# Chunk attention and a Fourier mix beside an MLP: weighting of v and the next tile's scores behind each other

## The chip, the cores and the metric

The kernel runs on one core of one Trainium2 chip. The metric is the device time of one execution in microseconds (us), as a median over several executions. All executions spoken of here were in the fast state. An engine is called by the profile's name where a line is read: PE is TensorE, DVE VectorE, ACT ScalarE, POOL GpSimd, SP SyncE.

## The reference

```python
q, k, v: [8, 8, 576, 64]                        # batch, heads, sequence, head dimension
# attention inside chunks of 64 positions (9 chunks)
scores = scale * q_c @ k_c.T;  scores -= max(scores)
attn = exp(scores);  attn /= sum(attn) + 1e-9
x = (attn @ v_c)  ->  [8, 576, 512]             # heads side by side
# Fourier mix and MLP
u  = x + real(fft(fft(x, axis=1), axis=2))
un = (u - mean(u)) / sqrt(var(u) + 1e-6)        # over the last axis
return u + relu(un @ w_ch1) @ w_ch2             # 512 -> 2048 -> 512
```

## The kernel before

The 4608 rows form 36 tiles of 128 rows. The MLP works on groups of four tiles (0 to 8). Its large products fill TensorE; the attention and the Fourier mix of the next batch run as a *side*, a generator of *steps*. After each *tick* of the MLP loop (16 matmul records of 128x128 by 256, some 3.45 us) the loop takes as many steps as the plan of that batch says. From group 2 on, the first product is computed in halves with seven products instead of eight. The last evictions of one tick free the bank into which the next tick writes, so a late VectorE is a late TensorE (at 464.93 us, 1.04 us of idle time).

```python
def attention(b):
    lo, hi = first[b], first[b + 1] - 1
    ...
    for n in range(lo, hi + 1):
        att_S(n)                   # scores: 32 matmuls of 64x64
        softmax(n)                 # DVE: maximum, subtraction; ACT: exponential
        yield
        if n + 1 < NT and (b > 0 or n < hi):
            att_T(n + 1)           # q and k of the next tile transposed in blocks by DVE
        yield
        if n > lo:
            att_V(n - 1)           # weighting of v: 32 matmuls of 64x64
            if n + 2 < NT:
                load_v(n + 2)
            yield ready(n - 1)
        att_P(n)                   # probabilities transposed by PE, copied by ACT
        yield
    att_V(hi)
    ...

def att_T(n):
    if n >= first[2]:
        for src, dst, nm in ((qs, qT, "qT"), (ks, kT, "kT")):
            a = src.pop(n)...
            t = one_p.tile([128, NJ, 2, CH + 1], FP32, tag=nm, name=nm)
            ...
            nc.vector.transpose(out=to..., in_=a)
        if n + 1 < NT:
            load(n + 1)            # q and k of the tile after it: one buffer each, just read
        return
    ...
```

`load` starts four transfers for q and four for k, or eight and eight where the two halves of a tile come from two batches, all on SyncE's queue. That queue also carries the loads of v, the fetches of weight slabs and this exchange of the first rows of a batch's tiles, whose second half waits until its first half has landed (1.51 us at one place):

```python
def shift(b):
    ...
    eng = nc.gpsimd if b < 2 else nc.sync
    t = three_p.tile([128, XW], FP32, tag="y", name="first")
    for i in range(NM):
        eng.dma_start(out=t[2 * i:2 * i + 2, 0:DM], in_=lows[i][0:CH + 1:CH, 0:DM])
    eng.dma_start(out=t[2 * NM:2 * NM + 1, 0:DM], in_=rest)
    for i in range(NM):
        eng.dma_start(out=lows[i][0:CH + 1:CH, 0:DM], in_=t[2 * i + 1:2 * i + 3, 0:DM])
    eng.dma_start(out=rest, in_=t[0:1, 0:DM])
```

The kernel's PSUM tiles take eight banks: two for transposes, two for one attention tile (scores or weighted tile), four for the MLP's products.

Of the kernel before, what the change touches and what calls it, by code (L numbers as in the profile page):

```python
# [16 lines left out]
def kernel(  # L17
# [32 lines left out]
    nc = tc.nc  # L50
# [230 lines left out]
            free.remove(fit[0])  # L281
            nc.sync.dma_start(out=raw(i).rearrange("p f r -> p (f r)"), in_=pieces[i][1].bitcast(U32))

    def round_weight(i):






        if i < len(pieces):
            w, t = pieces[i][0], raw(i)
            lo, hi, wi = t[:, :, 0], t[:, :, 1], w.bitcast(U32)
            p = power[i] = three_p.tile([128, 512], U32, tag="o", name="power")
            nc.vector.tensor_scalar(wi, hi, 0x000FFFFF, None, ALU.bitwise_and)
            nc.scalar.activation(out=w, in_=wi, func=ACTF.Copy, scale=2.0 ** -20, bias=1.0)
            nc.vector.tensor_scalar(p, hi, 0x7FF00000, None, ALU.bitwise_and)
            nc.scalar.activation(out=p, in_=p, func=ACTF.Relu, scale=-1.0, bias=top[:, 0:1])
            nc.scalar.activation(out=p, in_=p, func=ACTF.Relu, scale=-8.0, bias=top[:, 1:2])
        if 0 < i <= len(pieces):  # L300
            w, t = pieces[i - 1][0], raw(i - 1)
            lo, hi = t[:, :, 0], t[:, :, 1]
            p = power.pop(i - 1)
            nc.vector.scalar_tensor_tensor(w, lo, 2.0 ** -52, w, ALU.mult, ALU.add)
            nc.vector.scalar_tensor_tensor(p, hi, 0x80000000, p, ALU.bitwise_and, ALU.bitwise_or)
            nc.vector.tensor_tensor(out=w, in0=w, in1=p.bitcast(FP32), op=ALU.mult)
            r = raws.pop(i - 1)
            if i - 1 + len(spaces) < N_EARLY or r < N_LATE:
                free.append(r)
            load_weight(max(raws, default=i - 1) + 1)  # L310
# [6 lines left out]
        return pt  # L317


    def att_T(n):  # L320




        if n >= first[2]:
            for src, dst, nm in ((qs, qT, "qT"), (ks, kT, "kT")):
                a = src.pop(n).rearrange("p j (t b d) -> p j t b d", t=4, b=2)[:, :, :, 0]
                t = one_p.tile([128, NJ, 2, CH + 1], FP32, tag=nm, name=nm)
                low = kind(n) == LO and nm == "qT"
                to = t[:, :, :, CH:0:-1] if low else t[:, :, :, 0:CH]  # L330
                if kind(n) == HI:
                    to = to[:, :, ::-1]
                nc.vector.transpose(out=to.rearrange("p j c (r t) -> p j t c r", t=4), in_=a)
                if low:
                    nc.gpsimd.tensor_copy(t[:, :, :, 0:1], t[:, :, :, CH:CH + 1])
                dst[n] = t.rearrange("p j c t -> p (j c) t")
            if n + 1 < NT:
                load(n + 1)
            return
        a = qs.pop(n)  # L340
        pt = turn(lambda j: a[:, 2 * j:2 * j + 2, :].rearrange("p h d -> p (h d)"))
        t = one_p.tile([128, 2 * NJ, CH + 1], FP32, tag="qT", name="qT")
        low = kind(n) == LO
        nc.scalar.copy(t[:, :, CH:0:-1] if low else t[:, :, 0:CH], pt.rearrange("p j (c t) -> p (j c) t", c=2))
        if low and n < first[1]:
            nc.scalar.copy(t[:, :, 0:1], t[:, :, CH:CH + 1])
        elif low:
            nc.gpsimd.tensor_copy(t[:, :, 0:1], t[:, :, CH:CH + 1])
        qT[n] = t
        a2 = ks.pop(n)  # L350
        pt = turn(lambda j: a2[:, 2 * j:2 * j + 2, :].rearrange("p h d -> p (h d)"))
        t = one_p.tile([128, NJ, 128], FP32, tag="kT", name="kT")
        nc.scalar.copy(t, pt)
        kT[n] = t.rearrange("p j (c t) -> p (j c) t", c=2)
        if first[1] <= n + 1 < NT:
            load(n + 1)
# [17 lines left out]
    def softmax(n):  # L374
        sc = scs.pop(n)
        s4 = sc[:, :, 0:NJ * CH].rearrange("p e (j k) -> p e j k", j=NJ)
        mx = sm_p.tile([128, 2, NJ], FP32, tag="mx", name="mx")
        nc.vector.tensor_reduce(out=mx, in_=s4, axis=AX.X, op=ALU.max)
        ex = two_p.tile([128, NJ, 2, CH], FP32, tag="ex", name="ex")
        nc.vector.tensor_tensor(  # L380
            out=ex.rearrange("p j e k -> p e j k"),
            in0=s4,
            in1=mx.unsqueeze(3).to_broadcast([128, 2, NJ, CH]),
            op=ALU.subtract,
        )
        nc.scalar.activation(out=ex, in_=ex, func=ACTF.Exp, scale=scale)
        es[n] = ex

    def att_P(n):
        ex = es.pop(n)  # L390
# [5 lines left out]
    def att_V(n):  # L396
        a, b = pT.pop(n), vs.pop(n)
        if n < first[1]:
            xp = early_xp
        else:  # L400
            xp = ps_a.tile([128, 2, 512], FP32, tag="att", name="xp")
            xp = [xp[:, e] for e in range(2)], xp
        for j in range(NJ):
            for e in range(2):
                for c in range(2):
                    r0, t0 = e * CH, c * CH
                    nc.tensor.matmul(
                        out=xp[0][e][t0:t0 + CH, j * DV:(j + 1) * DV],
                        lhsT=a[r0:r0 + CH, j, t0:t0 + CH],
                        rhs=b[r0:r0 + CH, c, j, :],  # L410
                        start=True,
                        stop=True,
                    )
        x = xt(n)
        xo = x[:, DM:0:-1] if kind(n) == HI else x[:, 0:DM]
        xo = xo.rearrange("p (j e d) -> p e j d", j=NJ, e=2)
        rd = sm_p.tile([128, 2, NJ], FP32, tag="rd", name="rd")
        if n < first[1]:
            for e in range(2):
                nc.vector.tensor_scalar_add(rd[:, e], xp[0][e][:, D:NJ * DV:DV], 1e-9)  # L420
            nc.vector.reciprocal(out=rd, in_=rd)
            for e in range(2):
                xe = xp[0][e][:, 0:NJ * DV].rearrange("p (j d) -> p j d", j=NJ)
                nc.vector.tensor_tensor(
                    out=xo[:, e], in0=xe[:, :, 0:D], in1=rd[:, e].unsqueeze(2).to_broadcast([128, NJ, D]), op=ALU.mult,
                )
        else:
            xe = xp[1][:, :, 0:NJ * DV].rearrange("p e (j d) -> p e j d", j=NJ)
            nc.vector.tensor_scalar_add(rd, xe[:, :, :, D], 1e-9)
            nc.vector.reciprocal(out=rd, in_=rd)  # L430
            nc.vector.tensor_tensor(
                out=xo, in0=xe[:, :, :, 0:D], in1=rd.unsqueeze(3).to_broadcast([128, 2, NJ, D]), op=ALU.mult,
            )
        if kind(n) == HI:
            (nc.vector if n == at[HI, 0, 0] else nc.gpsimd).tensor_copy(x[:, 0:1], x[:, DM:DM + 1])
        elif kind(n) == RE:
            nc.gpsimd.memset(x[:, DM:DM + 1], 0.0)
# [68 lines left out]
    def attention_early():  # L506
# [32 lines left out]
        keep_warm(3)  # L539
        turn_tables()  # L540
        round_next()
        round_next()

    def attention(b):

        lo, hi = first[b], first[b + 1] - 1

        def ready(n):

            if n == at[LO, b, NM - 1]:  # L550
                shift(b)
            for i in range(NM):
                if n == at[HI, b, i]:
                    fold(b, i)
            if n == at[HI, b, 0]:
                fold(b, NM)
            return kind(n) == HI

        if b < 2:
            att_T(lo)  # L560
            yield
        for n in range(lo, hi + 1):
            att_S(n)
            softmax(n)
            yield
            if n + 1 < NT and (b > 0 or n < hi):
                att_T(n + 1)
            yield
            if n > lo:
                att_V(n - 1)  # L570
# [3 lines that stand above are left out]
            att_P(n)  # L574
            yield
        att_V(hi)
        if hi + 3 < NT:
            load_v(hi + 3)
        yield ready(hi)
# [341 lines left out]
    def down_plain(g, h1):  # L921
# [4 lines left out]
        for m in range(KF):  # L926
# [15 lines left out]
                    store(n, o)  # L942
            for j in range(G):
                due = KF - (G - j + 1)
                if m == due - 1:
                    normed(g + 1, j)
                if m == due:
                    turned(g + 1, j)
# [125 lines left out]
    with tc.manual_schedule():  # L1074
# [26 lines left out]
            for _ in range(times):  # L1101
                nc.tensor.matmul(out=idle[:, 0:NQ], lhsT=warm[:, 0:128], rhs=warm[:, 0:NQ], start=True, stop=True)

        def round_next():
            nonlocal n_w
            if n_w <= len(pieces):
                round_weight(n_w)
                n_w += 1

        keep_warm(8)  # L1110
# [2 lines left out]
        for step, _ in enumerate(fourier_early()):  # L1113
            if step == 0:
                turn_dim_tables()
        round_next()
        PAUSE = 3

# [7 lines left out]
        sizes = []  # L1126
        for b in range(1, B):
            n_tiles = first[b + 1] - first[b]
            sizes.append(4 * n_tiles + PAUSE + 2 + NM + b % 2 + (b == 1))
        done, cur = 0, 0  # L1130
        begin = [0]
        for g in range(NG):
# [96 lines left out]
```

## Time and profile before

| | before |
|---|---|
| median of 3 runs | 1122.93 us (1122.22 to 1128.66) |
| span of the profiled execution | 1122.2 us |
| mean granted TensorE clock | 0.999 of full speed |
| VectorE waiting for loads of q | 3.1 us, once |
| VectorE waiting for loads of k | 0.7 us, once |

The clock, a mean over the span, says that TensorE ran at full speed nearly throughout. The last two rows come from the view of waits. They are small, and they matter later. The lines on TensorE's own share, its groups and two of its stalls are in the prediction below.

### The profile page before, as it was taken

To read this page: it belongs to the slowest core of one execution; us is meant where nothing else is said; L and a number is where in the kernel's file an instruction comes from. 1 tells how busy PE (TensorE), PEld (TensorE's weight loads), DVE (VectorE), ACT (ScalarE), POOL (GpSimd) and SP (SyncE) were. 2 spreads that over 40 slices of the span, in tenths; PEclk is the share of its full clock that TensorE was granted. 3 is DMA by queue.
4 is the path that set the end of the run, shared out by engine and by line. 5 is a ranking of instruction groups with operands and counts; after the bars stand their busy time and mean duration, and the time that the engine had idled before them with its cause. 6 is when DMAs were issued, how large, how long until landed. Compare 5 with 4: busy or idle time off the path is not lost. (4 is left out here: it accounts for less than half of the span.)

```text
span 1122.2 us, 18759 instructions
## 1 busy us (share of the span) xinstructions
PE 1090.6 (97%) x7042; PEld 845.3 (75%) x7042; DVE 571.0 (51%) x1206; ACT 298.3 (27%) x725; POOL 276.3 (25%) x403
## 2 busy tenths in 40 slices
PE   8899999999999999999999999899999999999998
PEld 6544454446888888788888888778888888888887
DVE  4799987332555365563555355635454434323521
ACT  4688443221112311322122212221132102201210
POOL 4200003235404240063105230154024400130130
PEclk9999999999999999999999999999999999999999
DMA  8777647678475536772567356853654346446332
GB/s 171 226 195 180 158 147 236 179 233 294 149 226 163 160 137 215 213 212 79 177 194 214 114 178 199 226 157 110 194 199 113 113 144 204 141 149 195 89 113 75
DMA packets 147969, 192.72 MB, mean 172 GB/s; under 512 B 66126, under 2 KB 104014, under 8 KB 140712
## 3 DMA queue, kind: packets, MB, share of 16 engines
q1 hardware_dynamic: 145768, 190.46, 56.1%
q8 instruction: 56, 0.92, 0.3%
q0 software_dynamic: 512, 0.68, 0.3%
q10 hardware_dynamic: 1600, 0.39, 0.2%
q14 instruction: 33, 0.27, 0.1%
HBM read 167.22 MB, written 24.12 MB: 171 GB/s over the span
## 5 line engine op out<-in xcount | busy, mean ns | idle before, releaser
L880 POOL TENSOR_TENSOR h<-h 128x256 f32<-128x256 f32 x64 | 55.5, 873 | 412.7 <-PE pb L974 303.5
L1021 PE MATMUL pa<-wb,h 128*128 128x256 f32 x512 | 116.1, 381 | 0.0
L1021 PE MATMUL pb<-wb,h 128*128 128x256 f32 x512 | 115.0, 381 | 0.0
L974 PE MATMUL pb<-unT,wa 128*128 128x256 f32 x448 | 106.6, 381 | 4.1 <-DVE wa L983 4.1
L974 PE MATMUL pb<-wa 128*128 128x256 f32 x448 | 107.3, 382 | 1.1 <-DMA wa<-s 1.1
L974 PE MATMUL pa<-unT,wa 128*128 128x256 f32 x448 | 107.8, 383 | 0.0
L1021 PEld LDWEIGHTS pa<-wb,h 128*128 128x128 f32 x512 | 95.8, 190 | 14.6 <-issue 1.6
L1021 PEld LDWEIGHTS pb<-wb,h 128*128 128x128 f32 x512 | 95.8, 190 | 12.9
L974 PEld LDWEIGHTS pb<-unT,wa 128*128 128x128 f32 x448 | 84.3, 190 | 18.3 <-DVE wa L983 6.8
L974 PEld LDWEIGHTS pb<-wa 128*128 128x128 f32 x448 | 83.4, 190 | 14.3 <-DVE wa L981 1.5
L974 PEld LDWEIGHTS pa<-unT,wa 128*128 128x128 f32 x448 | 83.2, 190 | 11.6
L989 ACT ACTIVATE h<-pa 128x256 f32<-128x256 f32 x56 | 21.5, 383 | 176.1 <-PE pa L974 143.1
L890 PE MATMUL up<-unT,wa 128*128 128x512 f32 x128 | 58.0, 599 | 2.4 <-ACT h L898 1.6
L981 DVE TENSOR_TENSOR wa<-pa,wa 128x256 f32<-128x256 f32 x56 | 23.8, 425 | 70.6 <-PE pa L974 70.6
L928 PE MATMUL dn<-wb,h 128*128 128x512 f32 x128 | 57.7, 599 | 1.3 <-ACT h L898 1.3
L1021 PE MATMUL pa<-wb,yall 128*128 128x256 f32 x256 | 58.2, 382 | 0.0
L974 PE MATMUL pa<-wa 128*128 128x256 f32 x224 | 54.1, 384 | 3.8 <-ACT wa L979 3.8
L907 PE MATMUL up<-unT,wa 128*128 128x512 f32 x128 | 57.5, 598 | 0.0
L1021 PE MATMUL pb<-wb,yall 128*128 128x256 f32 x256 | 57.1, 380 | 0.0
L1021 PE MATMUL pb<-wb 128*128 128x256 f32 x256 | 56.6, 379 | 0.0
L1021 PEld LDWEIGHTS pb<-wb 128*128 128x128 f32 x256 | 48.2, 190 | 6.3
L1021 PEld LDWEIGHTS pa<-wb,yall 128*128 128x128 f32 x256 | 47.7, 190 | 6.9 <-issue 0.5
(233 smaller groups left out, 1646.0 us busy)
## 6 DMA issues: line engine op xcount, KB each, us to landing
wb<-s SPq DMA_DIRECT2D x56, 1024.0 KB
wa<-s SPq DMA_DIRECT2D x196, 256.0 KB
xall<-in_moe_w_ch_dram SPq DMA_DIRECT2D x22, 512.0 KB
q<-in_q_dram SPq DMA_DIRECT2D x96, 112.0 KB
k<-in_k_dram SPq DMA_DIRECT2D x96, 112.0 KB
v<-in_v_dram SPq DMA_DIRECT2D x124, 64.0 KB
yall<-in_moe_w_ch_dram SPq DMA_DIRECT2D x10, 512.0 KB
s<-wb SPq DMA_DIRECT2D x20, 256.0 KB
```

What stands on the lines that cost most here:

```text
L880: nc.gpsimd.tensor_tensor(out=h1[:, m, hi], in0=h1[:, m, lo], in1=h1[:, m, hi], op=ALU.subtract)
L890: nc.tensor.matmul(out=up, lhsT=w1[:, kk, m * 128:(m + 1) * 128], rhs=unT[:, kk], start=(kk == 0), stop=(kk == KD - 1),)
L907: nc.tensor.matmul(out=up, lhsT=w1[:, kk, m * 128:(m + 1) * 128], rhs=unT[:, kk], start=(kk == 0), stop=(kk == KD - 1),)
L928: nc.tensor.matmul(out=dn, lhsT=h1[:, m, s * 128:(s + 1) * 128], rhs=w2[:, m, :], start=(m == 0), stop=(m == KF - 1),)
L974: nc.tensor.matmul(out=dst, lhsT=w[:, kk, r], rhs=rhs[o][:, kk], start=(o in (0, 2) and kk == 0), stop=(kk == 1), skip_group_check=True,)
L981: nc.vector.tensor_tensor(out=b, in0=dst, in1=a, op=ALU.add)
L989: nc.scalar.activation(out=h1[:, m, lo], in_=dst, func=ACTF.Relu)
L1021: nc.tensor.matmul(out=dst, lhsT=lhs[:, m], rhs=w[:, m], start=(o in (0, 2) and m == 0), stop=(m == HF - 1), skip_group_check=True,)
```

## The change

For batches 2 to 7 the order of the steps is new. The weighting of tile n and the scores of tile n+1 stand in one step, so that TensorE changes between 128x128 and 64x64 matmuls once for both (0.10 us are lost on either side of a block in the kernel before). The exponential moves into the next step, the block transposes of q and k into one step each. Since scores and weighted tile now overlap in time, the weighted tile goes to the two banks of the transposes. A tile takes three steps instead of four. Besides, a normalisation in group 0 comes one tick earlier, and three activations of the early part are put off.

```diff
-    def att_T(n):
+    def att_T(n, which="qk"):
         if n >= first[2]:
             for src, dst, nm in ((qs, qT, "qT"), (ks, kT, "kT")):
+                if nm[0] not in which:
+                    continue
 ...
-            if n + 1 < NT:
+            if n + 1 < NT and "k" in which:
                 load(n + 1)
 ...
-        nc.scalar.activation(out=ex, in_=ex, func=ACTF.Exp, scale=scale)
         es[n] = ex
+        if n < first[2]:
+            exponential(n)
 ...
         if n < first[1]:
             xp = early_xp
+        elif n >= first[2]:
+            xp = [ps_t.tile([128, 512], FP32, tag="pt", name="xp") for _ in range(2)], None
 ...
+        if b > 1:
+            att_S(lo)
+            softmax(lo)
+            yield
+            for n in range(lo, hi + 1):
+                exponential(n)
+                if n + 1 < NT:
+                    att_T(n + 1, "q")
+                yield
+                att_P(n)
+                if n + 1 < NT:
+                    att_T(n + 1, "k")
+                yield
+                att_V(n)
+                if n < hi:
+                    att_S(n + 1)
+                    softmax(n + 1)
+                if n + 3 < NT:
+                    load_v(n + 3)
+                yield ready(n)
+            return
 ...
-                if m == due - 1:
+                if m == due - 2:
                     normed(g + 1, j)
 ...
-            sizes.append(4 * n_tiles + PAUSE + 2 + NM + b % 2 + (b == 1))
+            sizes.append((4 * n_tiles + 1 if b == 1 else 3 * n_tiles + 1) + PAUSE + 2 + NM + b % 2)
```

More of the change, by code (lines that the diff above doesn't have):

```diff
@@ L282, in load_weight, with round_weight @@
             nc.sync.dma_start(out=raw(i).rearrange("p f r -> p (f r)"), in_=pieces[i][1].bitcast(U32))
-    def round_weight(i):
+    def round_weight(i, later=None):
         if i < len(pieces):
@@ L294, in round_weight, with fraction, exponent @@
             p = power[i] = three_p.tile([128, 512], U32, tag="o", name="power")
+            def fraction(w=w, wi=wi):
+                nc.scalar.activation(out=w, in_=wi, func=ACTF.Copy, scale=2.0 ** -20, bias=1.0)
+            def exponent(p=p):
+                nc.scalar.activation(out=p, in_=p, func=ACTF.Relu, scale=-1.0, bias=top[:, 0:1])
+                nc.scalar.activation(out=p, in_=p, func=ACTF.Relu, scale=-8.0, bias=top[:, 1:2])
             nc.vector.tensor_scalar(wi, hi, 0x000FFFFF, None, ALU.bitwise_and)
-            nc.scalar.activation(out=w, in_=wi, func=ACTF.Copy, scale=2.0 ** -20, bias=1.0)
+            if later is None:
+                fraction()
             nc.vector.tensor_scalar(p, hi, 0x7FF00000, None, ALU.bitwise_and)
-            nc.scalar.activation(out=p, in_=p, func=ACTF.Relu, scale=-1.0, bias=top[:, 0:1])
-            nc.scalar.activation(out=p, in_=p, func=ACTF.Relu, scale=-8.0, bias=top[:, 1:2])
+            if later is None:
+                exponent()
+            else:
+                later += [fraction, exponent]
         if 0 < i <= len(pieces):
@@ L385, in softmax, with exponential @@
         )
-        nc.scalar.activation(out=ex, in_=ex, func=ACTF.Exp, scale=scale)
         es[n] = ex
+        if n < first[2]:
+            exponential(n)
+    def exponential(n):
+        nc.scalar.activation(out=es[n], in_=es[n], func=ACTF.Exp, scale=scale)
     def att_P(n):
@@ L417, in att_V @@
         rd = sm_p.tile([128, 2, NJ], FP32, tag="rd", name="rd")
-        if n < first[1]:
+        if xp[1] is None:
             for e in range(2):
@@ L541, in attention_early @@
         round_next()
-        round_next()
+        round_next(put_off)
     def attention(b):
@@ L557, in ready @@
             return kind(n) == HI
-        if b < 2:
-            att_T(lo)
+        if b > 1:
+            att_S(lo)
+            softmax(lo)
             yield
+            for n in range(lo, hi + 1):
[15 more added lines that the diff above has]
+            return
+        att_T(lo)
+        yield
         for n in range(lo, hi + 1):
@@ L565, in attention @@
             yield
-            if n + 1 < NT and (b > 0 or n < hi):
+            if n + 1 < NT:
                 att_T(n + 1)
@@ L1102, in keep_warm, with round_next @@
                 nc.tensor.matmul(out=idle[:, 0:NQ], lhsT=warm[:, 0:128], rhs=warm[:, 0:NQ], start=True, stop=True)
-        def round_next():
+        put_off = []
+        def round_next(later=None):
             nonlocal n_w
             if n_w <= len(pieces):
-                round_weight(n_w)
+                round_weight(n_w, later)
                 n_w += 1
@@ L1115 @@
                 turn_dim_tables()
+                for do in put_off:
+                    do()
         round_next()
```

## The prediction

> **What bounds the kernel now.** I read the page's busy shares first, then the chain that ended last, then the groups of TensorE by line, the waits, and the timeline around single steps.
>
> ```profile
> PE 1090.6 (97%) x7042; PEld 845.3 (75%) x7042; DVE 571.0 (51%) x1206; ACT 298.3 (27%) x725; POOL 276.3 (25%) x403
> ```
>
> TensorE (PE) is 97% busy, the next engine 51%. The chain that ended last lies on PE from 893 us to the end. So a change is worth only what it takes from PE's own time: 1122.2 - 1090.6 = 31.6 us in which PE is idle, and what is hidden in its busy time. Groups of PE by line (last column: idle before, and what ended it):
>
> ```profile
> L974 PE MATMUL pb<-unT,wa 128*128 128x256 f32 x448 | 106.6, 381 | 4.1 <-DVE wa L983 4.1
> L974 PE MATMUL pa<-wa 128*128 128x256 f32 x224 | 54.1, 384 | 3.8 <-ACT wa L979 3.8
> L604 PE MATMUL z<-tk,pm 128*128 128x289 f32 (+1 forms) x224 | 32.9, 317 | 2.6 <-POOL pm L495 1.7 <-ACT zr L632 0.8
> L365 PE MATMUL sc<-kT,qT 64*64 64x64 f32 x1152 | 25.0, 224 | 1.7 <-ACT kT L353 1.4
> L316 PE MATMUL pt<-ident,un 128*128 128x128 f32 x144 | 21.9, 274 | 3.4 <-ACT un L783 1.7 <-DVE un L785 1.7
> L407 PE MATMUL xp<-v,pT 64*64 64x65 f32 x992 | 21.6, 224 | 0.0
> ```
>
> These name the waits that matter. Two of them belong to steps that the change moves. The timeline shows the first, block transposes of q and k on DVE ahead of an eviction:
>
> ```profile
> 462.00 1.89 PE L974 MATMUL pb<-wa 128*128 128x256 f32 x8
> 462.62 1.10 DVE L333 STREAM_TRANSPOSE qT<-q 128x512 f32<-128x512 f32 x1
> 463.56 1.06 DVE L333 STREAM_TRANSPOSE kT<-k 128x512 f32<-128x512 f32 x1
> 464.47 0.73 DVE L983 TENSOR_TENSOR wa<-pb,wa 128x256 f32<-128x256 f32 x2
> 464.93 1.59 PEld L974 LDWEIGHTS pb<-unT,wa 128*128 128x128 f32 x8 [1.44 <-DVE wa L983]
> ```
>
> Eight matmul records take 8 x 0.216 = 1.73 us start to start, so the next product was due at 463.73 and came at 464.93: 1.2 us lost. The same stands at 481, 707 and 723 us. The second is the exponential, behind which a copy waits:
>
> ```profile
> 475.51 0.63 ACT L386 ACTIVATE ex<-ex 128x512 f32<-128x512 f32 x1 [1.02 <-DVE ex L380]
> 476.05 0.63 ACT L979 COPY wa<-pa 128x256 f32<-128x256 f32 x2
> 476.45 1.99 PE L974 MATMUL pa<-wa 128*128 128x256 f32 x8 [0.54 <-ACT wa L979]
> ```
>
> This stands seven times (326, 460, 476, 568, 702, 718, 810 us), 0.54 us idle each and 0.70 us by start-to-start times. The cost hidden in busy time is seen at a weighting step between large products:
>
> ```profile
> 600.38 1.89 PE L974 MATMUL pb<-unT,wa 128*128 128x256 f32 x8
> 602.20 0.70 PE L407 MATMUL xp<-v,pT 64*64 64x65 f32 x32
> 602.82 1.99 PE L974 MATMUL pa<-unT,wa 128*128 128x256 f32 x8
> 604.65 1.89 PE L974 MATMUL pb<-unT,wa 128*128 128x256 f32 x8
> ```
>
> 600.38 to 602.20 is 1.82 us where 1.73 is plain, and 602.82 to 604.65 is 1.83: 0.10 us lost on either side of each 64x64 block, scores alike. The block itself takes 0.62 us; its 32 records start over 0.48 us in steps of about 0.06 per four, so some 0.09 of the 0.62 is also the change back.
>
> [...] the 0.10 us on both sides stands around the 64x64 blocks, and 128x128 transposes between large products show none (0.44 us for four, nothing after). [...] the product into one half of pa waits for the copy of the other half, as the trace shows at 476.45. [...] I use start-to-start times.
>
> **The change, part by part.** Only batches 2 to 7 get the new order (27 tiles). I laid both orders of steps out by hand over the ticks of the matmul loop (16 ticks of the first product, 14 of the second per group), which tells what falls behind which product.
>
> *Removed.* (a) Within a batch the weighting of tile n and the scores of n+1 now follow each other: 27 - 6 = 21 pairs. A pair loses one change of mode each way: 0.10 + 0.10 + 0.09 = 0.29 us, 21 x 0.29 = 6.1 us. (b) The exponential is put into the next step, where its input is ready: 7 x 0.70 = 4.9 us. (c) The transposes of q and k stand in different steps: the four stalls of 1.2 us, 4.8 us. (d) In group 0 the normalisation goes one tick earlier; before, at 178.55 us, PE waited 1.74 for un (1.9 by starts): 1.9 us. (e) Batch 2 weights its last tile one tick (3.5 us) earlier, so the folding on POOL, for which PE waited 1.74 at 264.5, is done in time: 1.8 us. Sum 19.5 us.
>
> *Added.* (f) The weighted tile now takes both banks of the transposes' pair. In five groups, and once in group 0, the transposes of normalised tile 2 come in the same tick right before a weighting. Its second bank is then still being copied: the copy starts 0.67 us after those transposes start and takes 0.59 (290.97 to 291.56 after 290.30), PE can go on near 1.33 instead of 0.56. 0.77 x 5, and about 1.0 in the busier group 0: 4.9 us. (g) After the weighting, DVE now does two adds, a reciprocal and two multiplications (1.19 us in the early tiles with this form; one add and one multiplication took 1.05), then at once maximum and subtraction (2 x 0.72). It begins 0.81 us after the weighting starts, so DVE is free at 0.81 + 1.19 + 1.44 = 3.45 us. Where this falls before the eviction L983 (batches 3, 5, 7, one each) the third product starts at 3.9 instead of 3.0: 3 x 0.9 = 2.7 us. Where it falls before the last product of a pair (batches 4 and 6) the activations behind it delay the copy L979 by some 0.8: 1.6 us. (h) A q transpose alone before L983 still costs 0.27 (its successor starts 0.94 us later, so L983 at about 463.5 and PE at 464.0 instead of 463.73), and it falls there six times: 1.6 us. (i) Early part: putting off three activations (2.06 us) frees ACT before the first zf copy, but DVE's copy of the second quarter stays at 40.06 us behind its own rounding, so PE gains nothing; put after the zr copies they end near 44.7 and hold the Ln of the first statistics, which ran at 44.02: 0.6 us lost. (j) q and k of the next tile now have three ticks from issue to use, not four to five. In the trace they land 3.4 to 6 us after the last issue, against about 7 us left in the tightest place: 0.5 us for occasional lateness. Sum 11.9 us.
>
> Net 19.5 - 11.9 = 7.6 us: 1122.9 - 7.6 = 1115.3, said as 1115.
>
> **Rivals.** *The wait moves to the banks.* If (f) is larger, or also hits where I see one tick between (ACT busy with the previous copy), it eats the 6.1 us of (a) and more: 1120 to 1124. For it: two banks, three users. Against: apart from the six places a whole tick of 3.5 us lies between, and DVE needs 2 us. *Loads come late.* A q that lands late holds DVE, and behind it L983. Batch 2 before the change already has a 3.1 us wait of DVE for q, which cost PE nothing there; in the four tightest places of batches 4 and 6 it could cost 1 to 2 us each: 1119 to 1123. *Everything hidden.* If VectorE's longer work never delays PE and the banks are free in time, (f) and (g) vanish and the time is 1122.9 - 19.5 + 2.7 = 1106. For it: DVE is 51% busy. Against: L983 has only about 0.2 us of room, as 1.2 us lost to 2.1 us of transposes shows.
>
> **Range and chances.** The gains are seen in the trace, most of the losses are worked out from durations; I give the losses +-5 us and the gains +-3: 1109 to 1121. To be over 2% faster it would need under 1100.5, that is 22 us, more than all the gains that I count without any loss: 3%. Over 2% slower would need a new wait of 30 us, a late load in every tile: 2%.
>
> **What would show it.** Right: L407 directly before L365 21 times at about 0.54 us; no PE idle from L979 behind an exponential; the 1.2 us stalls at L983 gone, with 0.9 us ones after a weighting with scores in their place; PE idle at L407 released by ACT's copy unT L798, about 0.8 us six times; the idle from un L783 and pm L495 gone; up's first product at about 53 us instead of 52.5. Wrong: a new large idle released by a q or k load, by xall or by rd; a first product earlier than 52.5 us; the stalls of (b) back under another name.

## The result, and the profile after

The changed kernel takes 1132.24 us (1129.07 to 1132.77, six runs), the kernel before 1123.38 (1122.09 to 1128.66, six runs) in the same rounds. The ratio is 1.0068, with a 95% interval from 1.0044 to 1.0091: 0.7% slower. It lies within the 2% called the same, but outside the range, and the sign is wrong. A ratio, here and below, is the mean time of one kernel's fast runs over that of the other's of the same rounds, so it is not quite the ratio of the medians that are quoted.

First the page's busy time of the changed kernel:

```profile
PE 1090.8 (97%) x7042; PEld 851.1 (75%) x7042; DVE 583.4 (52%) x1260; ACT 297.9 (26%) x725; POOL 278.3 (25%) x403
```

PE's busy time is unchanged to 0.2 us, although pairs should have saved some; so something has lengthened matmuls elsewhere. The span is 1128.7 us, so PE is idle for 37.9 us instead of 31.6. The granted clock is 0.994 instead of 0.999. The groups of PE by line show where the idle time lies (the 7-product line is now L1015, last column idle time and its cause):

```profile
L1015 PE MATMUL pb<-wa 128*128 128x256 f32 x448 | 110.7, 391 | 6.0 <-DVE h L1032 6.0
L1015 PE MATMUL pb<-unT,wa 128*128 128x256 f32 x448 | 108.3, 385 | 10.1 <-DVE wa L1024 9.9
...
L1015 PE MATMUL pa<-wa 128*128 128x256 f32 x224 | 53.2, 380 | 0.7 <-ACT wa L1020 0.7
...
L426 PE MATMUL xp<-v,pT 64*64 64x65 f32 x992 | 23.5, 224 | 2.5 <-ACT unT L839 2.5
...
L327 PE MATMUL pt<-ident,un 128*128 128x128 f32 x144 | 21.8, 274 | 2.1 <-DVE un L826 2.1
```

The exponential's stall is nearly gone (third line), one of the two waits for a normalised tile too (last line). The bank wait of the weighted tile is there as predicted (fourth line). New are the first two: 16 us of waiting for evictions by DVE, where before had 4.1. The view of DVE's waits names a cause (total, number of waits, longest):

```profile
DVE qT L346 <- DMA q<-in_q_dram: 27.0, 8, 10.3
```

Some 19 us of these 27.0 lie in group 1, between 200 and 251 us, where PE does not depend on DVE so closely. The rest stands ahead of stalls of PE, but for 0.6 us, and so do two more waits of 3.4 us in all that the view puts down to k. The timeline of one of them (start, duration, engine and line; in brackets the idle time just before and its releaser; SPq is SyncE's queue):

```profile
332.83 1.12 DVE L346 STREAM_TRANSPOSE kT<-k 128x512 f32<-128x512 f32 x1
332.86 1.20 SPq L479 DMA_DIRECT2D first<-xall  x2
...
334.12 0.59 SPq L480 DMA_DIRECT2D first<-xall  x1
...
336.22 1.09 SPq L482 DMA_DIRECT2D xall<-first  x2
...
337.36 0.55 SPq L483 DMA_DIRECT2D xall<-first  x1
...
338.01 3.78 SPq L910 DMA_DIRECT2D wa<-s  x6
...
341.89 5.06 SPq L192 DMA_DIRECT2D q<-in_q_dram  x8
...
345.29 1.89 PE L1015 MATMUL pb<-unT,wa 128*128 128x256 f32 x8
...
348.88 1.09 DVE L346 STREAM_TRANSPOSE qT<-q 128x512 f32<-128x512 f32 x1 [1.89 <-DMA k<-in_k_dram]
349.81 0.74 DVE L1032 TENSOR_TENSOR h<-pb,wa 128x256 f32<-128x256 f32 x2
...
350.27 1.06 PE L1015 MATMUL pb<-wa 128*128 128x256 f32 x2 [3.09 <-DVE h L1032]
```

The program places the load right behind the transposes of k, which end at 333.95. On the queue, though, stand first the exchange of first rows (L479 to L483, 5.05 us, of which 1.51 us is the wait between its halves) and six slab fetches. The tile is one of those with eight transfers for q: the first is issued at 341.89, 7.94 us later, and the last is through at 346.95. DVE stands still for 1.89 us until q is there (the record names a load of k; those were issued from 347.05 on and are of no use to this transpose, so the late one is q's). Behind q's transposes stands the eviction L1032, and behind that PE: its next product was due 1.73 us after 345.29 and came at 350.27, 3.25 us too late.

What follows is in the view of stretches, here four of 3.41 us around this stall (busy time of PE, PE's weight loads, DVE, ACT and POOL, then the granted clock, the DMA share and GB/s):

```profile
343.64:347.06 3.42, 3.42 (x17) 2.78 (x15) 3.27 (x5) 0.77 (x2) 3.19 (x7) 1.00 0.73 211
347.06:350.47 3.41, 0.32 (x2) 0.20 (x2) 1.59 (x3) 0.22 (x1) 2.88 (x7) 1.00 0.42 104
350.47:353.89 3.42, 3.42 (x9) 2.60 (x9) 0.50 (x2) 1.16 (x3) 0.23 (x1) 0.50 0.69 221
353.89:357.30 3.41, 3.41 (x20) 3.00 (x19) 1.78 (x3) 1.75 (x4) 0.00 (x0) 1.00 0.78 196
```

In the stretch after the idle one the clock is 0.50, and PE does 9 matmuls there instead of 17 to 20. By start-to-start times that costs another 1.8 us, and it counts as busy time: this is part of what fills up PE's 1090.8. In this trace four stretches at half clock come before the end, each of 3.41 us: they start at 33.04, 350.48, 596.24 and 729.36 us, and their differences are 93, 72 and 39 times 3.4133 us. The stretch ahead of this one was not wholly idle: it had 0.32 us of work in it.

Six places have such a stall; by start-to-start times they cost (stall + half clock):

| at us | idle of DVE for q | PE late by | half clock |
|---|---|---|---|
| 350.27 | 1.89 | 3.25 | 1.8 |
| 468.40 | 3.45 | 3.81 | |
| 484.00 | 0.69 | 1.05 | |
| 596.39 | 1.47 | 2.85 | 1.7 |
| 711.85 | 0.85 | 1.21 | |
| 728.94 | 2.17 | 2.54 | 1.8 |

The sum is 14.7 + 5.3 = 20.0 us. Not all of it is due to the loads; the first experiment shows how much.

The bank wait, which was predicted, looks like this in the changed kernel's timeline, at 303 us:

```profile
303.49 0.60 PE L327 MATMUL pt<-ident,un 128*128 128x128 f32 x4
...
304.12 0.59 ACT L839 COPY unT<-pt 128x512 f32<-128x512 f32 x1 [3.31 <-PE pt L327]
...
304.76 0.62 PE L426 MATMUL xp<-v,pT 64*64 64x65 f32 x26 [0.41 <-ACT unT L839]
```

The weighting needs the bank that ACT still copies from; after its first few matmuls into the free bank it stands for 0.41 us.

### The profile page after: what moved, and what is told of

It reads as the page before. It is cut to its first block, busy times and chain, and to the rows that moved or that the text cites. A ratio compares the mean times of both kernels' runs of the same rounds, so it can differ in the third digit from the quotient of the medians.

```text
span 1128.7 us, 18810 instructions
## 1 busy us (share of the span) xinstructions
PE 1090.8 (97%) x7042; PEld 851.1 (75%) x7042; DVE 583.4 (52%) x1260; ACT 297.9 (26%) x725; POOL 278.3 (25%) x403
## 5 line engine op out<-in xcount | busy, mean ns | idle before, releaser
L1015 PE MATMUL pb<-unT,wa 128*128 128x256 f32 x448 | 108.3, 385 | 10.1 <-DVE wa L1024 9.9
L1015 PE MATMUL pb<-wa 128*128 128x256 f32 x448 | 110.7, 391 | 6.0 <-DVE h L1032 6.0
L1015 PE MATMUL pa<-unT,wa 128*128 128x256 f32 x448 | 106.6, 381 | 0.0
L1015 PEld LDWEIGHTS pb<-unT,wa 128*128 128x128 f32 x448 | 84.8, 191 | 25.7 <-DVE wa L1024 14.3
L1015 PEld LDWEIGHTS pb<-wa 128*128 128x128 f32 x448 | 85.4, 194 | 20.5 <-DVE h L1032 7.2
L1015 PEld LDWEIGHTS pa<-unT,wa 128*128 128x128 f32 x448 | 83.8, 190 | 11.2
L1015 PE MATMUL pa<-wa 128*128 128x256 f32 x224 | 53.2, 380 | 0.7 <-ACT wa L1020 0.7
L1062 PEld LDWEIGHTS pb<-wb,yall 128*128 128x128 f32 x256 | 48.1, 190 | 6.6
```

Source lines behind the costliest of these rows:

```text
L1015: nc.tensor.matmul(out=dst, lhsT=w[:, kk, r], rhs=rhs[o][:, kk], start=(o in (0, 2) and kk == 0), stop=(kk == 1), skip_group_check=True,)
L1062: nc.tensor.matmul(out=dst, lhsT=lhs[:, m], rhs=w[:, m], start=(o in (0, 2) and m == 0), stop=(m == HF - 1), skip_group_check=True,)
```

## The experiments

Two theories. **L, late loads:** with three steps per tile, and the load issued only after k's transposes, one step after q's, q has two steps from issue to use; what stands ahead on SyncE's queue uses them up, and DVE, PE and the clock follow. **B, banks and DVE's load:** the weighted tile in the transposes' banks and the long run of DVE work after a pair cost more than was worked out; the waits for q only fill time in which DVE would wait anyway. A side question, **E**, is whether the early part lost time.

A second buffer for q and k would have been the plain test. No such run is on record.

### no_loads: q and k loaded once, later tiles use the same data (wrong result on purpose)

```diff
     def load(n):
+        if n > first[2]:
+            qs[n], ks[n] = kept_qk
+            return
 ...
+                kept_qk.append(t)      # q and k of tile first[2]
```

> The changed kernel, but q and k are not loaded after the first tile of batch 2: later tiles use that tile's q and k again (wrong result on purpose). Theory L (late loads: VectorE waits in order for a q that has not landed, evictions stand behind it, TensorE idles and then gets half clock): no wait of VectorE for q or k, the idle times at 350, 468, 596, 712 and 729 us gone or at what the long VectorE work alone leaves (under 0.9 us), no half-clock interval in the middle; about 18 us less than the changed kernel, so 1111 to 1115 us. Rival B (the shared transposes' banks): nothing changes there, 1129 to 1132. Rival D (VectorE's longer work between weighting and subtraction): 1128 to 1132.

Measured: 1114.17 us (1112.50 to 1114.37, four runs), ratio 0.9910 (0.9893 to 0.9926), result wrong as intended. The six stalls are gone but for the 1.1 us of idle time (1.27 by starts) that the two at 350 and 596 keep at L1032. Those two come from DVE's work, not from loads. So late loads cost 14.7 - 2 x 1.27 + 5.3 = 17.5 us by the table; the two profiles differ by 1128.7 - 1112.6 = 16.1 us, the medians by 18.1. L holds, and B explains only the small rest. The kernel also moves fewer bytes, which this run does not separate; the next one does.

### split_loads: each load directly behind the transposes that empty its buffer

```diff
-    def load(n):
+    def load(n, which="qk"):
 ...
+            if nm not in which:
+                continue
 ...
-            if n + 1 < NT and "k" in which:
-                load(n + 1)
+            if n + 1 < NT:
+                load(n + 1, which)
```

> The changed kernel with the load of the next q issued right after q's block transposes, k's after k's, so that q has one step (3.5 to 5 us) more. Theory L: VectorE's wait for q falls from 27 us to under 10, TensorE's large idle times fall from about 3 us to under 1, so the half-clock intervals go too; 1114 to 1122 us. Rivals B and D: 1129 to 1132.

Measured: 1116.88 us (1114.38 to 1118.06, four runs), ratio 0.9934 (0.9915 to 0.9954), correct. Nothing but the place of q's load has changed, by one step. The groups of PE (lines are two higher):

```profile
L1017 PE MATMUL pb<-wa 128*128 128x256 f32 x448 | 107.5, 383 | 2.5 <-DVE h L1034 2.5
L1017 PE MATMUL pb<-unT,wa 128*128 128x256 f32 x448 | 107.0, 382 | 3.6 <-DVE wa L1026 3.3
```

Idle time fell from 6.0 and 10.1 to 2.5 and 3.6, and busy time from 110.7 and 108.3 to 107.5 and 107.0, as no stretch after the early part runs at half clock any more (the granted clock is 1.000). DVE's wait for q fell from 27.0 to 5.2 us. Its wait for k rose from 1.6 to 18.7 us (five waits), but 15.8 of these lie in group 1, between 205 and 252 us, and the two others, 1.1 and 1.9 us, before transposes at 350 and 591 us, bring back no stall of the table. So it is the time of the loads, not their bytes.

### turn2_earlier: transposes of normalised tile 2 in another tick than the weighting

```diff
-                        if k == 4 + 2 * j:
+                        if k == (4, 6, 7, 10)[j]:
                             normed(g + 1, j)
-                        if k == 5 + 2 * j:
+                        if k == (5, 7, 8, 11)[j]:
                             turned(g + 1, j)
```

> The changed kernel with the transposes of normalised tile 2 one half-step earlier (and its normalisation two), so that they don't stand right before a weighting that takes their bank. Theory L with a small part for the banks: the five waits of 0.41 us idle (0.73 by starts) at the weighting go, 3.7 us less than the changed kernel, 1126 to 1129; the waits for q stay. Rival B: 8 us or more less, 1123 or below. Nothing at all would say that the wait was hidden anyway.

Measured: 1128.35 us (1126.79 to 1129.49, four runs), ratio 1.0038 (1.0020 to 1.0056), correct. That is 3.9 us under the changed kernel. The idle time before the weighting fell from 2.5 to 0.4 us, the wait of group 0; the waits for q stayed (30.9 us). The bank wait is real and of the predicted size. It is not what made the kernel slow. (By the diff the normalisation of tile 2 moves by one half-step, not by two as the expectation says.)

### before_late: the kernel before, its loads two steps later

```diff
 # att_T
-            if n + 1 < NT:
-                load(n + 1)
 # attention, after att_P(n)
+            if first[2] <= n + 1 < NT - 1:
+                load(n + 2)
```

> The kernel before, its order of steps untouched, but the next tile's q and k are loaded two steps later (after the block transposes of the exponential instead of after those of q and k). Theory L: with two steps of lead VectorE waits for q by more than 20 us in all (before: 3.1), TensorE idles at L983 and L991; 1128 to 1138 us. Rivals B and D, for which the loads don't matter: 1122 to 1125.

Measured: 1168.01 us (1167.40 to 1169.99, four runs), ratio 1.0396 (1.0375 to 1.0418), correct. The expectation allowed for 5 to 15 us of loss; it is 45. DVE's waits:

```profile
DVE qT L333 <- DMA q<-in_q_dram: 46.3, 9, 11.4
DVE kT L333 <- DMA k<-in_k_dram: 14.3, 11, 4.1
```

With nothing of the change in it, the old kernel gets the same stalls at the same evictions (18.4 us at the first, 12.4 at a copy by ACT, where it had 4.1 and 3.8). Here k waits as well, since both loads are late and both transposes are in one step. The size can be added up from the profiles, which differ by 44.0 us: PE is idle for 59.7 us instead of 31.6, 7.4 of it at one weighting at 258 us in group 1; the stretches at half clock after the early part add up to 34.1 us (the granted clock is 0.984), PE works in 27.9 of them, so some 14 us are lost; and one in the early part costs 1.7. That makes 43.8. The expectation reckoned with neither so much idle time nor the half clock. The direction supports L; my size for it was off by a factor of three at least.

### split_turn2: both repairs

The edits of split_loads and turn2_earlier together.

> The split loads and the earlier transposes of tile 2 together. If the two causes add up: 1116.9 less 2.5 to 4.4 (five bank waits of 0.73 us by starts, and what turn2_earlier showed), 1112 to 1115 us. If the bank waits were hidden behind the late loads: 1116 to 1118.

Measured: 1113.37 us (1111.88 to 1114.88, six runs), ratio 0.9903 (0.9883 to 0.9923), correct. From 1132.24, the repairs alone took 15.4 and 3.9 us; together they took 18.9. They add up within the noise, so they are two separate costs.

### split_turn2_put: the same, the three early activations not put off

```diff
-        round_next(put_off)
+        round_next()
```

> As split_turn2, with the early rounding's ScalarE part not put off (as in the kernel before). The prediction's item (i) says that putting off costs 0.6 us: this one 0.6 us faster than split_turn2. The traces so far (first product at 52.4 us with it in split_loads, at 52.5 in the kernel before) say no difference over 0.2 us, and that the 1.3 us in the changed kernel's profile were a half-clock interval: same within 0.5 us.

Measured: 1112.39 us (1111.77 to 1114.08, six runs), ratio 0.9896 (0.9878 to 0.9914), correct. The intervals overlap, and the medians differ by 1.0 us. The first product of the MLP starts at 53.76 us in this profile and at 52.77 in that of split_turn2, but only this one had a half-clock stretch in the early part, and with one and the put-off it came at 53.85 to 54.62 in other runs. Without a stretch, the put-off kernels alone spread from 51.80 to 53.95. Inconclusive: whatever E is worth is not clear of the noise.

### shift_pool: the changed kernel, the exchange of first rows on GpSimd's queue

```diff
-        eng = nc.gpsimd if b < 2 else nc.sync
+        eng = nc.gpsimd
```

> The changed kernel with the exchange of first rows (the small transfers with a round trip, first<-xall and back) issued from GpSimd's queue instead of SyncE's for all batches. If SyncE's queue, in order, is part of why loads come late: the stalls at 350, 596 and 729 us, whose load stands behind such an exchange, shrink or go; those at 468 and 712 stay; 1117 to 1125 us. If the queue's order plays no part and only the number of steps does: 1129 to 1132.

Measured: 1117.97 us (1115.62 to 1120.18, four runs), ratio 0.9942 (0.9917 to 0.9966), correct: one line, 14.3 us. The timeline of the place that was shown above:

```profile
330.75 1.11 DVE L346 STREAM_TRANSPOSE kT<-k 128x512 f32<-128x512 f32 x1
...
334.31 4.71 SPq L192 DMA_DIRECT2D q<-in_q_dram  x8
```

From the end of k's transposes to the issue of q it now takes 2.45 us instead of 7.94. The stalls at 350, 596 and 729 are gone, and so is that at 484; what is left is 1.1 us once, at 588, from DVE's work. Those like 468 and 712, where other work stands ahead on the queue, are still there (2.76 us at 460.68, 2.27 at 703.34, with a half clock each; the granted clock is 0.996). DVE's waits for q still add up to 26.4 us, mostly in group 1: the total of a wait says little, its place says all.

What is saved at the place above is the 5.05 us for which the exchange held SyncE's queue, 3.5 of them for its six issues and 1.51 for the wait between its halves. That is not small where a load that is already late stands behind it: PE came 3.25 us too late there.

### split_turn2_shift: all three

> split_turn2 with the exchange on GpSimd's queue too. Little is left to gain on loads (VectorE's waits for k, 18.7 us, cost TensorE at most 1 us): 0 to 1 us less than split_turn2; or up to 2 us more, if GpSimd's folding behind the exchange then comes late for the Fourier product.

Measured: 1112.51 us (1111.45 to 1112.96, five runs), ratio 0.9891 (0.9872 to 0.9911), correct. Once q's load is in its right place, the exchange matters no more. This is the fastest version on record beside split_turn2_put, with which it overlaps: 1.1% under the kernel before.

### apart: split_turn2, but weighting and scores in steps of their own

```diff
                 att_V(n)
-                if n < hi:
-                    att_S(n + 1)
-                    softmax(n + 1)
                 if n + 3 < NT:
                     load_v(n + 3)
                 yield ready(n)
+                if n < hi:
+                    att_S(n + 1)
+                    softmax(n + 1)
+                    yield
 ...
-            sizes.append((4 * n_tiles + 1 if b == 1 else 3 * n_tiles + 1) + ...)
+            sizes.append((4 * n_tiles + 1 if b == 1 else 4 * n_tiles) + ...)
```

> split_turn2 with the scores of the next tile in a step of their own after the weighting (four steps a tile, as before, so that a large product stands between the two). What the pairs alone are worth: 21 pairs x 0.35 us (a lone block costs 0.82 us by starts in the traces so far, a pair 1.29) = 7.4 us lost; in return VectorE's work no longer comes in one piece and its stalls after a pair go (3 x 0.8 and 2 x 1.3 us = 5.0). So 2 to 3 us more than split_turn2, 1114 to 1117; the trace should show the two terms separately. If the pairs were worth nothing: 1108 to 1110. If VectorE's stalls stay: 1119 to 1121.

Measured: 1123.34 us (1121.11 to 1124.07, five runs), ratio 0.9992 (0.9978 to 1.0005), correct. It should tell what the pair itself is worth, and missed its expectation by over 6 us. The stalls of DVE's work after a pair are gone, as expected. But the timeline has a new one:

```profile
239.08 1.22 SPq L481 DMA_DIRECT2D first<-xall  x2
...
247.27 0.58 DVE L922 TENSOR_TENSOR wb<-h 128x256 f32<-128x256 f32 x1 [11.50 <-DMA s<-wb]
...
250.36 1.11 PE L329 MATMUL pt<-ident,ex 128*128 128x128 f32 x4 [6.08 <-ACT ex L406]
```

The exchange fell into another tick, stores of prepared weights stood behind it on SyncE's queue, DVE waited 11.50 us for one of them, and PE 6.08 us behind DVE. Two stretches at half clock, 6.8 us from 247.4 us on, go with it (the granted clock is 0.995); 2.96 us of them lie in the idle time itself, so some 1.9 us are lost. The order of steps alone moved a wait. Also, the weighting is again in a tick with the transposes of normalised tile 2, and five bank waits of 0.41 us idle are back, which turn2_earlier had removed. The run does not give the price of the pair.

### apart_shift: the same, the exchange on GpSimd's queue

The edit of shift_pool on top of apart.

> apart with the exchange of first rows on GpSimd's queue, as in split_turn2_shift. apart was 10 us slower than expected because of one idle time of 6.1 us at 250 us with a half-clock interval behind it: VectorE waited 11.5 us for stores of rounded weights that stood in SyncE's queue behind the exchange. If that is right the stall goes, and the rest of apart's trace (from 260 us on it lost only 2.3 us on split_turn2) holds: 1112 to 1115 us. If not: 1121 to 1124.

Measured: 1118.41 us (1116.18 to 1121.36, six runs), ratio 0.9947 (0.9926 to 0.9967), correct. The stall at 250 shrank to 1.88 us, at 246, without half clock. The run still lies 3.4 us above its range. Beside split_turn2_shift its last matmul comes 7.45 us later (medians 5.9 apart). The groups of PE show what I had left out, first split_turn2_shift, then this run:

```profile
L428 PE MATMUL xp<-v,pT 64*64 64x65 f32 x992 | 21.9, 224 | 0.4 <-ACT unT L841 0.4
L428 PE MATMUL xp<-v,pT 64*64 64x65 f32 x992 | 23.5, 224 | 2.5 <-ACT unT L842 2.5
```

The five bank waits, 0.73 us each by starts, are back, as in apart: 3.7 us. The sum from the traces is 7.4 for the pairs (a lone block still costs 0.82), 3.7 for the banks and 1.9 for the stall at 246, less 6.0 for DVE's stalls after a pair, which are all gone: 7.0 of the 7.45 us. So an estimate for the pairs net of the DVE stalls that they cause is 7.4 - 6.0 = 1.4 us. No run isolates it, as both runs without pairs moved the weighting back to the banks.

### before_shift: the kernel before, the exchange on GpSimd's queue

The same edit in before.

> The kernel before with the exchange on GpSimd's queue. Before the change the loads land in time (VectorE waits 3.1 us for q, TensorE not at all), so the queue should matter little: 1121 to 1124 us. If it is faster by more than 4 us, the gain of the last kernels is not a repair of the change but one of its own.

Measured: 1120.97 us (1120.30 to 1121.81, four runs), ratio 0.9968 (0.9950 to 0.9986), correct. A part of the gain could have come from before's own waits. It is small: 0.3%, a hair below the expected range, and in the profile it is the folding's wait at 264 us (1.74 us idle) and two waits for weight slabs (1.1), against 1.3% in the changed kernel. So the 14.3 us of shift_pool are mended lateness, not a general gain.

## Why the prediction was wrong

| step of the prediction | said, us | the runs showed |
|---|---|---|
| (a) pairs | 6.1 | lone blocks cost 0.82 by starts, pairs 1.29: 2 x 0.82 - 1.29 = 0.35 each, x 21 = 7.4. Right. |
| (b) exponential | 4.9 | idle behind it gone; the 0.7 of idle time left at this copy belongs to (g). Right. |
| (c) q and k in different steps | 4.8 | the four stalls of two transposes are gone; the same eviction now waits behind late q. Right, undone by (j). |
| (d), (e) earlier normalisation, folding | 1.9, 1.8 | idle for the normalised tile 3.4 to 2.1, folding's 1.7 gone: 1.3 and 1.7. Right, (d) a little large. |
| (f) banks | 4.9 | 2.02 - 1.29 = 0.73 per place, six places: 4.4. Right. |
| (g) DVE after a pair | 4.3 | 0.81 at three places, 0.53 at two: 3.5; missed: 1.27 at two more, where DVE's backlog reaches the next step with q's transposes. 6.0 in all. |
| (h) one transpose before L983 | 1.6 | in no_loads six times 0.28 to 0.29: 1.7. Right; in the changed kernel mostly inside the late loads. |
| (i) early part | 0.6 | the first product came 1.34 later in one profile with an early half-clock stretch; not resolved. |
| (j) loads | 0.5 | 16 to 18. **The step that failed.** |

Step (j) named the right thing and mis-sized it some thirty times. It counted three ticks from where the load stands in the program, and compared them with the landing time after the *last* issue. Both ends were wrong. The load is issued one step after q's buffer is free, so q has two steps, not three. And between the end of k's transposes, behind which the program has the load, and its first issue lie 3.4 to 7.9 us of queue at the six stalls. The rival "loads come late" had the mechanism and the places (batches 4 and 6 among them), with 1 to 2 us each. What it lacked is that a stretch at half clock follows three of the six late evictions and costs 1.7 to 1.8 us each, and that the exchange of first rows holds the queue for 4.1 to 6.5 us once per batch.

Without (j), the working stands: it gives 19.5 - 11.4 = 8.1 us of gain, and no_loads against before gives 1122.2 - 1112.6 = 9.6 in the profiles. The terms of the table as measured, with (b) and (c) as said and 1.34 for (i), make 20.1 - 13.4 = 6.7. Of the 2.9 us left, 1.2 (by starts) are two waits for weight slabs, at 356.89 and 598.58 us, which the kernel before has and no_loads has not; they were in no term. The other 1.7 us I cannot assign. The idea itself earns little: against the 7.4 us of (a) stand 10.4 of (f) and (g), which come with it; what is gained comes from (b) to (e), and turn2_earlier takes most of (f) back.

Of what was to show it wrong, "a new large idle released by a q or k load" came, through DVE. The sentence that DVE is 51% busy, put there for the rival that all is hidden, is no measure of this: DVE's mean is 52% in the changed kernel too, and one wait of 3.45 us in its queue makes PE 3.81 us late.

What stays open: the early part, and 1.7 us of the sum.

## What to carry to other kernels

When a loop gets fewer steps per tile, count the lead of each load anew, from the moment its queue gets to it, with everything that stands ahead on that queue (here 7.94 us at one place); and issue each load right behind the last reader of its own buffer, not behind that of its neighbour (15.4 us in split_loads). Keep small transfers, above all those that wait for others, off the queue that carries loads with little lead (here they held it for 5.05 us at one place). Where a late load holds an engine, ask which eviction stands behind it, as L1032 stood behind q's transposes on DVE here (PE 3.25 us late), and look for a half clock behind the stall: here three of six stalls, with PE late by 2.54 to 3.25 us, cost another 1.7 to 1.8 us in that way, and one of 3.81 us did not.

## What the traces show of clock, queue and change of mode

- The four half-clock stretches of the changed kernel's trace before its end last 3.41 us each and start whole multiples of that length apart (93, 72 and 39). Cut into intervals of this length, the trace has four with 2.22, 2.37, 2.53 and 3.09 us of idle time of PE in them; each was followed by one at half clock, though none was idle throughout. The others before the end have up to 1.87 us, and after them the clock stayed full, also where a gap straddles two intervals (3.65 us, at 468 us, as 1.78 + 1.87). So what a stall cost on top differed in this trace: 1.7 to 1.8 us, or nothing.
- Moving the six small transfers of the exchange, which held SyncE's queue for 5.05 us at one place, to GpSimd's took 14.3 us off the changed kernel (1132.24 to 1117.97) and about 3 us off the kernel before.
- 0.10 us are lost on either side of a block of 64x64 matmuls here, and merging two blocks of 32 saved 0.35 us.
- 7.94 us lay at one place between the end of the transposes behind which the program places the load and its first issue.
